# Starts of weight and moving tiles in SBUF: one residue of 256 bytes against all of them for weights

## The chip, the cores and the metric

The kernel runs on one core of a Trainium2 chip. The metric is the device time of one execution in microseconds (us). PE is TensorE, DVE is VectorE, ACT is ScalarE, POOL is GpSimd; SP issues DMAs. PEld is the weight load that precedes each matmul; on its row of the profile it lies beside the matmuls.

## The reference

Three stages in float32, each on the output of the one before:

```python
# q, k, v: 4 batches x 12 heads x 448 x 64
scores = scale * np.matmul(q, k.transpose(0, 1, 3, 2)) - np.log(S)
attn = 1.0 / (1.0 + np.exp(-scores))
x = np.matmul(attn, v)                     # then laid out as 1792 x 768
h = np.maximum(np.maximum(x @ w1, x @ w2), x @ w3)     # 768 x 768 each
y = h @ moe_w_out                                      # 768 x 768
z = y @ w_in                                           # 768 x 2048
g = np.maximum(z, 0.0) + alpha * np.minimum(z, 0.0)
out = g @ moe2_w_out                                   # 2048 x 768
```

## The kernel before

Everything is held transposed: a tile has 128 features on the partitions and 448 tokens along them. Attention (L563 and L584) runs first, as 64x64 tiles of float32. All that follows, 3,528 matmuls at L694, is one form: a weight block of 128x128 and a moving block of 128x448.

Two things make these blocks. First, each product of block matrices is done in Strassen's manner (the Winograd form): sums and differences of weight quarters and of token quarters are formed on VectorE, and seven products k = 0 to 6 take the place of eight. Second, each operand is cut into a high part (a rounded copy, name ending in h) and a low part (the rest, in l), both float32r, and a product is three matmuls: low weights by high moving, high by low, high by high. `split_ops` (L296) makes the pair, `product` (L855) and `e_group` (L1255) issue the matmuls. Weight parts are `f` (made from `weights`, 128x384 for three blocks), `cf` (stored in attention's time and loaded back, for `moe_w_out`) and, in the last stage, `lf`. Moving parts are `x`, `h`, `y` and, in the last stage, `rf`. The matmuls up to about 641 us on the profile's clock are the middle stages (names `u_`), the rest the last one (`eX`, `eV`, `eW`).

Vector and scalar work is not issued where it is written but by a list of operations: `advance` is called after each group of matmuls and issues what is ready and has credit. Its rules are numbers of columns, not addresses.

Where the tiles lie is what the change is about. Pools are stacks in SBUF, from the left (constants, `wpool`, then `slots_a`, in whose place `slots_l` comes for the last stage) and from the right (`edge`, then attention's `apool`, in whose place `slots_c` and then `slots_e` come). Tiles of 448 float32 are 1,792 bytes (7 x 256), tiles of 384 are 1,536 bytes (6 x 256), and a block of 128 inside one is 512 bytes further on. So with the pads of `pad` (L97: 48 words ahead of the first slot of `slots_a`, 16 words behind the slots on the right, 48 words ahead of the moving tiles of `slots_l`) every weight block of L694 starts at byte 0 and every moving block at byte 192, counted modulo 256. Attention's operands all start at byte 0.

`wslot` (L111) gives the 21 buffers of tag `ws` in turn: words as loaded, sums, and `f` and `cf` parts. `tile_l` (L1064) gives the tiles of the last stage, the sixteen of tag `lf` among them; the last stage's even-numbered weight parts come from `wslot`, its odd ones from tag `lf`. A pool that takes the place of another (`reuse_waits="tile"`) makes an instruction wait for the last use of the tiles that its own tile lies over.

Of the kernel before, what the change touches and what calls it, by code (L numbers as in the profile page):

```python
# [16 lines left out]
P = 128  # L17
# [45 lines left out]
def kernel(  # L63
# [19 lines left out]
    HF = HK * P  # L83
# [6 lines left out]
    wpool = ctx.enter_context(tc.tile_pool(name="wpool", bufs=1))  # L90
    dpool = ctx.enter_context(tc.tile_pool(name="store", bufs=1, space=bass.MemoryType.DRAM))
    pools = {}
# [4 lines left out]
    def pad(pool, w):  # L97

        if pool not in padded:
            padded.add(pool)  # L100
            pools[pool].tile([P, w], F32, tag="pad", name=f"pad_{pool}")

    def slot(nm, pool="a", w=TW, dt=F32):
        if pool == "a":
            pad(pool, 48)
        t = pools[pool].tile([P, w], dt, tag="s" + pool, name=nm, bufs=room[pool])
        if pool != "a":
            pad(pool, 16)
        return t

    def wslot(nm, dt=F32, pool="w"):  # L111

        if pool != "w":
            return slot(nm, pool, HF, dt)
        return wpool.tile([P, HF], dt, tag="ws", name=nm, bufs=21)

# [134 lines left out]
    def word_ops(z, gate=None, early=False):  # L253
# [4 lines left out]
        def first():  # L258
            st["r"] = wraw.pop(z)
            st["T"] = wslot(f"wt{z}", U32)  # L260
            if not early:
                nc.scalar.activation(  # L262
                    st["T"].bitcast(F32), st["r"][:, :, 1].bitcast(F32), AF.Abs, scale=2.0**-112
                )
            nc.scalar.activation(st["r"][:, :, 0], st["r"][:, :, 0], AF.Copy, scale=2.0**-29)  # L265
# [53 lines left out]
    def words_via(z):  # L319


        d = dpool.tile([P, HF], F32, tag=f"wv{z}", name=f"wv{z}")

        stored = store_word(z, lambda: d)

        def back(gate):
            def load():
                word[z] = wslot(f"wb{z}")
                nc.sync.dma_start(out=word[z], in_=d)

            return op("Q", 0, load, stored, gate=gate, lag=2)

        return back

    def unit_ops(u, z, gates=None, words=word_ops, store=False, engine="A"):
# [10 lines left out]
        def sum1():  # L346
            t["s"] = wslot(f"wu{u}")
            tensor_op(t["s"], word[z + 2], word[z + 3], ALU.add)
# [65 lines left out]
    def forms(q, of, into, homes, soon=False):  # L414
# [10 lines left out]
        def cut(c, x, *deps):  # L425
            def make(y):
                if y == "h":
                    home[c] = homes(c, 2)
                    take(home[c], 2)
                    if into is hf:  # L430
                        hhome[g, c, r] = home[c]
                return slot(f"{q}_{c}{y}", home[c], TW, F32R)

            o = split_ops(
                into[g, c, r], make, lambda: b[x][0], TW, *deps, gate=lambda: homes(c, 2), soon=soon
            )
            if (c, x) not in ((2, "T"), (1, "21")):
                o.after.append(lambda: used(x))
            return o

        def t1():
            p = homes(None, 1)
            take(p)
            b["T"] = slot(f"{q}_t", p), p
            tensor_op(b["T"][0], b["12"][0], b["11"][0], ALU.subtract)
            used("11")
# [610 lines left out]
    def ff3(ps_m, dpool, fd, wd, slopes, seq, turn_left):  # L1057
# [3 lines left out]
        lf, rf = ({(k, kp): {} for k in range(7 * n) for kp in range(KP)} for n in (1, 2))  # L1061
        sums, held, firsts, pair = {}, {}, [], {}

        def tile_l(tag, nm, w, bufs, dt=F32):  # L1064
            return pools["l"].tile([P, w], dt, tag=tag, name=nm, bufs=bufs)

        def load_op(homes, make, src, gate, lag):
# [23 lines left out]
        def load_w(k, kp, n):  # L1091


            nm = f"wl{k}_{kp}_{n}"

            def make(h):
                if h == "wr":
                    if kp % 2 == 0:
                        pair[kp // 2] = wpool.tile([P, HF, 2], F32, tag="wr", name=nm, bufs=4)
                    x = pair[kp // 2].rearrange("p f t -> p (f t)")  # L1100
                    return x[:, kp % 2 * HF : (kp % 2 + 1) * HF]
                if h == "wf":
                    x = wpool.tile([P, HF, 2], F32, tag="wr", name=nm, bufs=4)
                    return x.rearrange("p f t -> p (f t)")[:, :HF]
                return wslot(nm) if h == "ws" else tile_l("wl", nm, HF, 4)

            def gate():
                if k == 0:
                    return kp // 2 in pair if kp % 2 else free["wr"] > 1
                return "l" in pools  # L1110

            return load_op(("wr",) if k == 0 else ("wl", "ws", "wf"), make, lambda: wd[kp, n], gate, 8 if k else 2)

        def load_g(n, kp, what):
            nm = f"gl{n}_{kp}_{what[0]}{what[1]}"
            key = what, n % 2, kp
            return load_op(

                ("rr", "e") if n else ("a",),
                lambda h: tile_l("rr", nm, TW, 14) if h == "rr" else slot(nm, h),  # L1120
                lambda: fd[key], lambda: (not n or "l" in pools) and key in fd,
                8 if n else 1,
            )
# [4 lines left out]
        def left_ops(k, kp):  # L1128

            if k == 2:  # L1130
                (a, o, end_a), (b, p, end_b) = load_w(k, kp, 1), load_w(k, kp, 3)
                c = sums[kp] = {}

                def add():
                    c["x"] = tile_l("wsum", f"ws{kp}", HF, KP)
                    tensor_op(c["x"], a["x"], b["x"], ALU.add)

                o = op("D", HF, add, o, p, lag=2)
                end_a(o), end_b(o)
            elif k == 3:  # L1140
                (a, o, end_a), (c, p, end) = load_w(k, kp, 0), load_w(k, kp, 1)
                s = sums[kp]
                sums[k, kp] = sum_op(s, s, a, ALU.subtract, HF, o, maker[id(lf[2, kp])])
                o = sum_op(c, a, c, ALU.subtract, HF, p, sums[k, kp])
                end_a(o)
            elif k == 4:
                c, o = sums[kp], sums[3, kp]
            else:
                c, o, end = load_w(k, kp, (0, 2, None, None, None, 3, 2)[k])
                if k == 6:  # L1150
                    o = sum_op(c, c, sums[kp], ALU.subtract, HF, o)
# [261 lines left out]
```

## Time and profile before

| | |
|---|---|
| median of 2 runs | 851.16 us (850.94 to 851.38) |
| profiled execution | 851.17 us, span of the trace 849.3 us |
| PE busy | 844.4 us (99%) |
| PEld busy | 732.8 us (86%) |
| DVE, ACT, POOL busy | 655.4, 517.7, 146.9 us (77, 61, 17%) |
| HBM traffic | 200 GB/s over the span |

In the page's second part each digit is the busy tenth of a fortieth of the span: PE stands at 9 throughout but for the last slice, and so does the granted clock. The chain of work that ended last is followed back from the last instruction to what released it. A busy PE is not PE at its peak, because ends of matmuls are modelled; what tells the pace is the distance from one start to the next.

### The profile page before, as it was taken

How to read it: one execution, taken by the hardware profiler on the slowest of the kernel's cores; microseconds unless marked ns; L12 is line 12 of the kernel's file. 1: busy time of each engine (PE TensorE's matmuls, PEld its weight loads, DVE VectorE, ACT ScalarE, POOL GpSimd, SP SyncE). 2: the span in 40 equal slices, each digit the busy share in tenths (PEclk: the TensorE clock that was granted, in tenths of full speed). 3: DMA queues.
4: the chain of work that ended last, by engine and by line, in shares of the span. 5: the costliest groups of instructions: out<-in, count | busy, mean ns of one | idle time of the engine just before them, and what ended most of it. 6: DMA issues, size and time to landing. Idle time of an engine off the chain costs nothing.

```text
span 849.3 us, 14230 instructions
## 1 busy us (share of the span) xinstructions
PE 844.4 (99%) x4878; PEld 732.8 (86%) x4878; DVE 655.4 (77%) x1304; ACT 517.7 (61%) x1006; POOL 146.9 (17%) x272
## 2 busy tenths in 40 slices
PE   9999999999999999999999999999999999999998
PEld 4444678999999999999999999999999999999997
DVE  1889888789979988797488988977768687868631
ACT  6888997644655464656377867776657554453530
POOL 1464000003200312410001322221211010001110
PEclk9999999999999999999999999999999999999999
DMA  7899632445845765987531766534547999437111
GB/s 269 277 371 350 214 110 87 131 135 191 284 155 159 240 207 171 360 314 222 157 95 65 243 196 232 184 131 155 172 162 265 328 351 371 144 118 242 69 44 54
DMA packets 77863, 170.45 MB, mean 201 GB/s; under 512 B 11120, under 2 KB 51856, under 8 KB 77792
## 3 DMA queue, kind: packets, MB, share of 16 engines
q1 hardware_dynamic: 60048, 106.38, 39.7%
q0 software_dynamic: 17456, 62.83, 19.6%
q8 instruction: 38, 0.62, 0.3%
q10 hardware_dynamic: 288, 0.34, 0.1%
q14 instruction: 33, 0.27, 0.1%
HBM read 123.12 MB, written 46.40 MB: 200 GB/s over the span
## 4 chain that ended last, share of the span: by engine, by line
PE 99%; DVE 0%; ACT 0%; issue 0%
PE u_0X L694 17%; PE u_1X L694 17%; PE eW L694 10%; PE eX L694 10%; PE u_1W L694 9%; PE u_0W L694 9%; PE sc L563 8%; PE pav L584 7%; PE u_0V L694 4%; PE u_1V L694 4%; PE eV L694 3%; PE warm L629 0%; DVE o L1232 0%; ACT o L1230 0%; DVE zeros L625 0%
## 5 line engine op out<-in xcount | busy, mean ns | idle before, releaser
L571 ACT ACTIVATE a<-sc,bias_s 128x896 f32<-128x896 f32 x84 | 83.2, 1010 | 12.7 <-PE sc L563 11.6
L563 PE MATMUL sc<-qt,kt 64*64 64x448 f32 x672 | 83.1, 540 | 0.0
L584 PE MATMUL pav<-a,vt 64*64 64x448 f32 x672 | 82.0, 536 | 0.0
L281 DVE CUSTOM_DVE_ANT_0 wt<-wr,wt 128x768 uint16<-128x768 uint16 x112 | 62.6, 559 | 3.9
L273 DVE SCALAR_TENSOR_TENSOR wr<-wr 128x384 uint32<-128x384 uint32 x112 | 62.0, 554 | 0.4
L265 ACT ACTIVATE wr<-wr 128x384 uint32<-128x384 uint32 x112 | 62.1, 554 | 0.0
L563 PEld LDWEIGHTS sc<-qt,kt 64*64 64x64 f32 x672 | 36.3, 134 | 29.3 <-issue 14.8
L584 PEld LDWEIGHTS pav<-a,vt 64*64 64x64 f32 x672 | 35.9, 133 | 28.1 <-issue 19.1
L262 ACT ACTIVATE wt<-wr 128x384 f32<-128x384 f32 x92 | 51.0, 554 | 14.7 <-DMA wr<-in_weights_dram 11.6
L741 DVE SCALAR_TENSOR_TENSOR r<-n,nalpha,r 128x448 f32<-128x448 f32 x64 | 42.8, 682 | 14.5 <-ACT n L738 14.4
L774 POOL DMA_DIRECT2D gd<-r x48 | 25.9, 541 | 159.6 <-DVE r L741 145.2
L245 POOL DMA_DIRECT2D wd<-wt x32 | 17.7, 553 | 174.4 <-DVE wt L281 173.6
L889 ACT COPY u<-u_1X 128x448 f32<-128x448 f32 x40 | 21.3, 533 | 38.5 <-PE u_1X L694 38.4
L272 DVE TENSOR_SCALAR wt<-wt 128x384 uint32<-128x384 uint32 x112 | 39.8, 355 | 5.5 <-ACT wt L262 4.8
L889 ACT COPY u<-u_0X 128x448 f32<-128x448 f32 x40 | 21.3, 533 | 35.6 <-PE u_0X L694 35.5
L874 ACT COPY u_0V<-u_0X 128x448 f32<-128x448 f32 x20 | 10.3, 518 | 48.0 <-PE u_0X L694 48.0
L311 DVE TENSOR_TENSOR u<-u_1W,u 128x448 f32<-128x448 f32 x34 | 21.2, 623 | 23.8 <-ACT u L889 19.5
L311 DVE TENSOR_TENSOR u<-u_0W,u 128x448 f32<-128x448 f32 x34 | 21.2, 623 | 18.3 <-ACT u L889 14.4
L1287 ACT COPY p<-eW 128x448 f32<-128x448 f32 x12 | 6.4, 534 | 34.1 <-PE eW L694 34.1
L599 DVE COPY x<-pav 128x448 f32<-128x448 f32 x12 | 7.5, 624 | 22.3 <-PE pav L584 22.3
L737 ACT ACTIVATE r<-u 128x448 f32<-128x448 f32 x32 | 18.5, 579 | 5.6 <-DVE u L311 5.6
L311 DVE TENSOR_TENSOR p<-eX,p 128x448 f32<-128x448 f32 x12 | 7.5, 623 | 16.4 <-PE eX L694 16.4
(821 smaller groups left out, 2791.7 us busy)
## 6 DMA issues: line engine op xcount, KB each, us to landing
wr<-in_weights_dram SPq DMA_DIRECT2D x100, 384.0 KB, 3.6
gl<-gd SPq DMA_DIRECT2D x79, 224.0 KB, 4.4
wl<-wd SPq DMA_DIRECT2D x64, 192.0 KB, 4.5
gd<-r POOLq DMA_DIRECT2D x48, 224.0 KB, 2.7
gl_T<-gdT SPq DMA_DIRECT2D x32, 224.0 KB, 5.1
hr<-hd POOLq DMA_DIRECT2D x28, 224.0 KB, 5.9
wd<-wt POOLq DMA_DIRECT2D x32, 192.0 KB, 3.8
kt<-in_k_dram SPq DMA_DIRECT2D x23, 224.0 KB, 5.3
```

The lines of the kernel that those rows point to most:

```text
L262: nc.scalar.activation(st["T"].bitcast(F32), st["r"][:, :, 1].bitcast(F32), AF.Abs, scale=2.0**-112)
L265: nc.scalar.activation(st["r"][:, :, 0], st["r"][:, :, 0], AF.Copy, scale=2.0**-29)
L272: nc.vector.tensor_scalar(st["T"], st["T"], 3, None, ALU.logical_shift_left)
L273: nc.vector.scalar_tensor_tensor(out=st["r"][:, :, 0], in0=st["r"][:, :, 1], scalar=0x80000000, in1=st["r"][:, :, 0], op0=ALU.bitwise_and, ...
L281: nc.vector.tensor_tensor(out=st["T"], in0=st["r"][:, :, 0], in1=st["T"], op=ALU.add)
L311: nc.vector.tensor_tensor(out=out, in0=a, in1=b, op=op)
L563: nc.tensor.matmul(sc[g * KH : (g + 1) * KH, j, :S], keys[u, z][r, m * KH : (m + 1) * KH], queries[u, z][r], start=True, stop=True,)
L571: nc.scalar.activation(a, sc[:, :, :S], AF.Sigmoid, bias=bias_s, scale=scale)
L584: nc.tensor.matmul(pv[key][j * D : (j + 1) * D, :S], vts[u][r, m, j], a[r, j], start=start, stop=stop,)
L694: nc.tensor.matmul(ps[:, : rh.shape[-1]], lt, rh, start=(start and z == 0), stop=(stop and z == len(mms) - 1), skip_group_check=True,)
L741: nc.vector.scalar_tensor_tensor(out=s["r"], in0=s["n"], scalar=nalpha[:, f : f + 1], in1=s["r"], op0=ALU.mult, op1=ALU.add,)
L889: nc.scalar.copy(side[u, g, k], banks[X][:, :TW])
```

## The change

Tiles of tag `ws` and of tag `lf` become 8 words (32 bytes) longer, and what is used of such a tile begins at word 0, 1, ... 7 in turn, by a counter that all of them share. With the longer tiles the buffers themselves begin at all multiples of 32 bytes modulo 256, so that the 128-column weight blocks of L694 begin at all multiples of 4 bytes, a quarter of them at multiples of 16. The pads are altered: moving blocks begin at byte 64 in the middle stages and at byte 96 in the last. What is computed, by which instructions and in which order, stays. Attention's operands still begin at byte 0.

```diff
--- before.py
+++ after.py
@@ -102,17 +102,25 @@
 
     def slot(nm, pool="a", w=TW, dt=F32):
         if pool == "a":
-            pad(pool, 48)
+            pad(pool, 40)
         t = pools[pool].tile([P, w], dt, tag="s" + pool, name=nm, bufs=room[pool])
         if pool != "a":
-            pad(pool, 16)
+            pad(pool, 48 if pool == "c" else 40)
         return t
+
+    turn = [0]
+
+    def shifted(pool, tag, w, dt, nm, bufs):
+
+        c = turn[0] % 8
+        turn[0] += 1
+        return pool.tile([P, w + 8], dt, tag=tag, name=nm, bufs=bufs)[:, c : c + w]
 
     def wslot(nm, dt=F32, pool="w"):
 
         if pool != "w":
             return slot(nm, pool, HF, dt)
-        return wpool.tile([P, HF], dt, tag="ws", name=nm, bufs=21)
+        return shifted(wpool, "ws", HF, dt, nm, 21)
 
 
 
@@ -1062,6 +1070,8 @@
         sums, held, firsts, pair = {}, {}, [], {}
 
         def tile_l(tag, nm, w, bufs, dt=F32):
+            if tag == "lf":
+                return shifted(pools["l"], tag, w, dt, nm, bufs)
             return pools["l"].tile([P, w], dt, tag=tag, name=nm, bufs=bufs)
 
         def load_op(homes, make, src, gate, lag):
```

No row changes its place on any engine. What differs are some waits, because tiles of the last stage lie over other tiles of the middle stages than before. The place that tells most is SP's queue where the last stage's pool is taken into use (`gl` are stored activations, `wl` weight words, both loaded back for the last stage; in square brackets the semaphores, PE_49 being PE's). Before:

```order
L1084 DMA gl1_0_00_7529<-gd00_1_0_5370 128x448 [waits DMAHW1_49,PE_49]
L1084 DMA gl1_1_00_7534<-gd00_1_1_5696 128x448 [waits DMAHW2_49]
L1084 DMA gl1_2_00_7539<-gd00_1_2_5989 128x448 [waits DMASW4_49,DMAHW3_49,DMASW2_49,DVE_49]
L1084 DMA gl1_3_00_7544<-gd00_1_3_6292 128x448 [waits DMAHW4_49]
L1084 DMA gl1_4_00_7549<-gd00_1_4_6573 128x448 [waits DMAHW5_49,DMASW0_49]
L1084 DMA gl1_5_00_7554<-gd00_1_5_6850 128x448 [waits DMAHW6_49,DMASW2_49]
L1084 DMA gl1_6_00_7559<-gd00_1_6_7119 128x448 [waits DMAHW0_49,DMAHW7_49,DMASW4_49,DVE_49]
L1084 DMA gl1_7_00_7564<-gd00_1_7_7347 128x448 [waits DMASW4_49]
...
L1084 DMA wl1_6_2_7622<-wd62_5654 128x384 [waits DMAHW7_49]
L1084 DMA wl1_7_2_7631<-wd72_6118 128x384 [waits DMAHW0_49]
L1084 DMA wl2_2_1_7812<-wd21_2474 128x384 [waits DMAHW5_49]
```

After the change:

```order
L1094 DMA gl1_0_00_7529<-gd00_1_0_5370 128x448 [waits DMAHW1_49,PE_49]
L1094 DMA gl1_1_00_7534<-gd00_1_1_5696 128x448 [waits DMAHW2_49,DMAHW5_49,DVE_49,PE_49]
L1094 DMA gl1_2_00_7539<-gd00_1_2_5989 128x448 [waits DMAHW3_49]
L1094 DMA gl1_3_00_7544<-gd00_1_3_6292 128x448 [waits DMAHW4_49,DMASW4_49,DMASW2_49]
L1094 DMA gl1_4_00_7549<-gd00_1_4_6573 128x448 [waits DMASW0_49]
L1094 DMA gl1_5_00_7554<-gd00_1_5_6850 128x448 [waits DMAHW6_49,DMASW2_49]
L1094 DMA gl1_6_00_7559<-gd00_1_6_7119 128x448 [waits DMAHW7_49,DMASW4_49,PE_49]
L1094 DMA gl1_7_00_7564<-gd00_1_7_7347 128x448 [waits DMAHW0_49,DMASW4_49]
...
L1094 DMA wl1_6_2_7622<-wd62_5654 128x384 [waits DMAHW7_49,PE_49]
L1094 DMA wl1_7_2_7631<-wd72_6118 128x384 [waits DMAHW0_49,PE_49]
L1094 DMA wl2_2_1_7812<-wd21_2474 128x384 [waits DMAHW5_49,PE_49]
```

Before, the one wait for PE is that of gl1_0, and it is for the last matmul of u16_0W. With the change, the program's counts say, gl1_0 waits for a matmul of u16_0V, 18 counts earlier, five more loads wait for PE, each for a later count than the one before it, and the last, wl2_2, for the same count as gl1_0 before.

## Rows read from the trace of the kernel before

**Rows 1.** The page: busy us and share by engine; the chain that ended last.
```profile
PE 844.4 (99%) x4878; PEld 732.8 (86%) x4878; DVE 655.4 (77%) x1304; ACT 517.7 (61%) x1006; POOL 146.9 (17%) x272
...
PE 99%; DVE 0%; ACT 0%; issue 0%
```

**Rows 2.** Waits of PE: who for whom, us in total, times, longest.
```profile
PE warm L629 <- DVE zeros L625: 1.2, 1, 1.2
```

**Rows 3.** Timeline of the end, all engines: start, length, instruction.
```profile
845.26 0.37 PE L694 MATMUL eW<-rf_7h,lf_7h 128*128 128x448 f32 x1
845.66 0.35 ACT L1230 COPY o<-eW 128x224 f32<-128x224 f32 x1 [26.92 <-PE eW L694]
...
846.04 0.39 DVE L1232 COPY o<-eW 128x224 f32<-128x224 f32 x1 [4.61 <-ACT o L1230]
846.46 0.34 SPq L1225 DMA_DIRECT2D out_dram<-o  x1
```

**Rows 4.** The chain in order of time: start, length, line, instructions.
```profile
1.22 2.74 PE warm L629 x6
...
127.47 0.75 PE sc L563 x8
128.22 0.75 PE pav L584 x8
...
467.06 3.64 PE u_1W L694 x18
...
641.78 29.12 PE eX L694 x144
...
758.26 58.24 PE eX L694 x288
```

**Rows 5.** The page, costliest groups: attention matmuls, count, busy us, mean ns.
```profile
L563 PE MATMUL sc<-qt,kt 64*64 64x448 f32 x672 | 83.1, 540 | 0.0
L584 PE MATMUL pav<-a,vt 64*64 64x448 f32 x672 | 82.0, 536 | 0.0
```

**Rows 6.** Stretches: us; busy us of PE, PEld, DVE, ACT, POOL; clock, DMA share, GB/s.
```profile
75.00:230.00 155.00, 155.00 (x1093) 127.41 (x1086) 133.49 (x277) 109.28 (x197) 19.13 (x35) 1.00 0.54 174
230.00:480.00 250.00, 250.00 (x1238) 231.73 (x1237) 202.87 (x399) 144.88 (x306) 38.65 (x71) 1.00 0.61 197
580.00:750.00 170.00, 170.00 (x842) 157.61 (x841) 129.46 (x244) 100.08 (x210) 19.49 (x36) 1.00 0.69 237
```

**Rows 7.** Timeline of PE where attention ends.
```profile
131.91 0.47 PE L694 MATMUL u_0X<-x_0h,f_0l 128*128 128x448 f32 x1
132.23 0.36 PE L694 MATMUL u_0X<-x_0l,f_0h 128*128 128x448 f32 x1
132.43 0.36 PE L694 MATMUL u_0X<-x_0h,f_0l 128*128 128x448 f32 x1
132.63 0.37 PE L694 MATMUL u_0X<-x_0l,f_0h 128*128 128x448 f32 x1
132.83 0.56 PE L694 MATMUL u_0X<-x_0h,f_0h 128*128 128x448 f32 x2
```

**Rows 8.** Timeline of the weight loads at the same place.
```profile
132.23 0.19 PEld L694 LDWEIGHTS u_0X<-x_0h,f_0l 128*128 128x128 f32 x1
132.43 0.19 PEld L694 LDWEIGHTS u_0X<-x_0l,f_0h 128*128 128x128 f32 x1
132.63 0.39 PEld L694 LDWEIGHTS u_0X<-x_0h,f_0h 128*128 128x128 f32 x2
```

**Rows 9.** Last stage, tile eX: count, ns min/median/max, first and last start.
```profile
L694 PE MATMUL eX<-rf_0h,lf_0l x18: 367/368/368, 641.6 to 811.5; 128*128 128x448 f32 x18
L694 PEld LDWEIGHTS eX<-rf_0l,lf_0h x18: 187/188/188, 641.6 to 811.5; 128*128 128x128 f32 x18
L694 PE MATMUL eX<-rf_0l,lf_0h x18: 361/361/361, 641.8 to 811.7; 128*128 128x448 f32 x18
...
L694 PE MATMUL eX<-rf_0h,lf_0h x18: 363/363/363, 642.0 to 811.9; 128*128 128x448 f32 x18
```

**Rows 10.** The page, DMA issues: count, KB each, median us to landing.
```profile
wl<-wd SPq DMA_DIRECT2D x64, 192.0 KB, 4.5
...
wd<-wt POOLq DMA_DIRECT2D x32, 192.0 KB, 3.8
```

**Rows 11.** Waits on SP's DMA queue: us in total, times, longest.
```profile
SPq L1084 <- PE u_0W L694: 21.0, 1, 21.0
```

## The prediction

> **What bounds the kernel now.** I read the share of busy time first: PE is busy for 844.4 of 849.3 us [rows 1]. A busy share can hide waits, so the list of waits came next: the only thing that PE ever waited for is the zeroing of its warm-up block, 1.2 us at the start [rows 2]. The chain of work that ended last then says the same of the end: PE holds 99% of it [rows 1], and behind the last matmul, which starts at 845.26 us, only two copies of 0.35 and 0.39 us and the output's last transfers remain [rows 3]. So the time is a sum of matmul spacings, and an edit counts only if it alters the spacing, or if it makes PE wait where it does not now.
>
> Which spacings? In attention the chain shows eight matmuls in 0.75 us, again and again [rows 4]. From 131.91 us on [rows 7] all 3,528 matmuls (the 4,878 of rows 1 less twice 672 of attention [rows 5] and 6 of the warm-up [rows 4]) are of one form, 128x128 weights against 448 columns. The chain gives 18 in 3.64 us in the middle, 144 in 29.12 and 288 in 58.24 us in the last stage [rows 4]: 202.2 ns each, the same everywhere, whatever VectorE, ScalarE and the DMAs do meanwhile. 3,528 x 202.2 = 713.4 us, and 131.9 + 713.4 = 845.3 us, where the last one begins. The sum closes; there is no other term.
>
> The granted clock is 1.00 in these stretches [rows 6], that is the 2.4 GHz level. 448 columns at 2.4 GHz are 186.7 ns, so 15.5 ns of each spacing (54.7 us in all) are not columns. Two views say what they might be. A weight load begins with each matmul and runs under it: the loads stand at the same hundredths of a us as the matmuls before theirs, 132.23, 132.43, 132.63 [rows 7, 8]. And the recorded matmul durations come in a beat of three, 368, 361 and 363 ns for the three products of a triple, hardly a ns of spread in 18 of each [rows 9]. Durations here are spacing plus a constant, so their distances from their mean, 364, put the spacings at an estimated 206.2, 199.2 and 201.2 ns. Nothing outside PE has such a beat. I read it as the stream of moving columns and the stream of weights getting in each other's way, at phases that repeat because every weight row begins at byte 0 and every moving row at byte 192, counted modulo 256.
>
> **The change part by part.** Order and number of instructions stay. (1) Attention's tiles keep their addresses (they are laid from the other end of the memory), so its 131.9 us stay: 0. (2) Moving rows still begin at one residue each, 64, in the last stage 96. (3) Weight rows begin at any word. Parts 2 and 3 act on one number, the mean spacing, 3.53 us of the total for each ns. The kernel before has one pair of residues only, so no row shows another, and the price has to be bounded. From below: 186.7 ns, no excess left, -54.7 us, 796.5 us; a floor, since every last stall would have to come from these addresses. From above: the heaviest step of the beat every time, 206.2 ns, 4.0 x 3.528 = +14.1 us, 865 us; no row excludes more, since no word-shifted row is in the trace. Between these ends the nearest rows are the first spacings of the stage, before the beat has settled: the starts 132.23, 132.43, 132.63 and 132.83 [rows 7] are three spacings in 0.60 us, 200 ns with an error of some 3 ns from the hundredths. A phase off the beat thus costs about what the beat costs, and I take 202.2 ns: 0 us.
>
> The Trainium skill speaks against part 3: SBUF — State Buffer, Specifications, gives cachelines of 16 bytes and a penalty for each cross to a new line. Three quarters of the word starts are off a 16-byte line, and a 512-byte weight row from there touches 33 lines and not 32; as an estimate from that page, a 32nd of the 15.5 ns in three quarters of the loads is 0.36 ns, or +1.3 us. No row of the kernel before has such a load.
>
> (4) Other engines and DMAs read and write the shifted tiles. What hides a loss there is that PE waits for none of them. In the densest stretch, 75 to 230 us, VectorE is busy 133.5 of 155 us [rows 6]; its work would have to grow by 16% before it binds by busy time. DMAs of weights land in some 4 to 5 us [rows 10]; if their cover went, the loss would be such a landing at the head of a stage, a few us. I put 0. (5) The new addresses move some waits, since a tile of the last stage now lies over other tiles of the stage before. On SP's queue gl1_0 waits 21.0 us for a matmul on u_0W [rows 11], with all further loads queued behind it. In the change's program the wait of gl1_0 is for an earlier matmul; gl1_1, gl1_6, wl1_6 and wl1_7 wait for later ones in turn, and the old one stands 36 rows further on, at wl2_2. So SP's loads go out no later than now, and nobody on the path waited for them: 0.
>
> Sum: 849.3 us of span + 0, and 851.17 - 849.3 = 1.9 us around it: 851 us. The profiled execution (851.17) is as good as the median of the two shown (851.16).
>
> **The rivals.** Faster, the beat breaks to the good. For it: the heavy step returns every third time because nothing varies; with varied starts the dear phase might be left. If only the other two steps remained, the mean were 200.2 ns, -7.1 us, 844 us; if half of the 15.5 ns went, -27 us, 824 us. Against it: the unsettled spacings are no cheaper than the rest by more than their error [rows 7]. It decides below 197.4 ns, where 17 us (2%) are gained.
>
> Slower, shifted weight loads stall the stream more. For it: a fixed pattern can be one that has settled into few collisions, and shifted rows never let it settle. The heavy step every time gives 865 us; 868 us need 207.0 ns, 4.8 over now, a third more stall than today. Against it: the mean would have to pass the worst step on record.
>
> Nothing happens: the address does not matter, and the 15.5 ns are the load's own pace; 851 us with the same beat of 368, 361, 363 ns. For it: loads of 187 to 188 ns [rows 9] that start with the matmul before end close to the next one's start, and the beat is the same for all tiles, wherever in memory they lie. Against it: a plain hand-over between load and matmul has no reason to repeat only after three. The Trainium skill has this as a rule (SBUF — State Buffer, Who interferes with whom): PE reads the moving operand and the weights over two independent ports and never waits on anyone. By it the change does nothing; the trace, 202.2 against 186.7 ns, agrees only if the excess is no conflict.
>
> **How the numbers follow.** Mean spacing as now within about 1.5 ns, in another beat: 0.44 (846 to 856 us). No effect whatever: 0.10. Faster by more than that: 0.27, of which 0.17 beyond 2%. Slower by more: 0.19, of which 0.12 beyond 2% (shifted DMAs that at last make PE wait are in it with 0.03). Two per cent are about what a measurement of this kernel can tell from no change. So faster 0.17, same 0.44 + 0.10 + 0.10 + 0.07 = 0.71, slower 0.12. For the range I cut 0.10 on either side: 828 us (195.6 ns) to 870 us (207.5 ns).
>
> **What would show it.** In the chain's rows after: eight attention matmuls still in 0.75 us; 144 matmuls of the last stage in 29.1 us if I am right, in 28.4 or less for the faster rival at 2%, in 29.8 or more for the slower. The three durations should no longer be 368, 361 and 363 with hardly a spread: if they are, the third rival holds. Moving rows at 64 and at 96 should differ little, middle and last stage keeping one mean. PE's list of waits should still hold the 1.2 us of the warm-up alone; a DMA or VectorE there would make steps 4 or 5 wrong. A mean more than 5 ns off 202 would make the step from three unsettled spacings to "a phase off the beat costs the same" the wrong one.

## The result: 0.6% slower, and every added microsecond is matmul spacing

| | before | after |
|---|---|---|
| median | 851.16 us | 856.61 us |
| ratio to before | | 1.0063, 95% interval 1.0043 to 1.0083 |
| span of the profiled execution | 849.3 us | 854.7 us |

Forecast were 851 us and no change. By the medians the kernel became 5.45 us slower. That is only 0.6%, but the interval lies wholly above 1. The prediction took two per cent for about what a measurement of this kernel can tell from no change; this one tells 0.2% to either side.

The page after the change, part 1, and its chain by engine (they answer to [rows 1]):

```profile
PE 849.7 (99%) x4878; PEld 731.8 (86%) x4878; DVE 655.7 (77%) x1304; ACT 518.9 (61%) x1006; POOL 147.1 (17%) x272
...
PE 99%; DVE 0%; ACT 0%; issue 0%
```

PE's waits in the same trace (they answer to [rows 2]):

```profile
PE warm L637 <- DVE zeros L633: 1.2, 1, 1.2
```

So PE still waits for nothing after its warm-up. VectorE's busy time went from 655.4 to 655.7 us; reading and writing tiles that start at odd words cost it nothing that shows.

The chain in order of time, of attention's end and of the last stage (start, length, line, number of matmuls; it answers to [rows 4]):

```profile
128.97 0.75 PE sc L571 x8
...
645.51 29.26 PE eX L702 x144
674.77 29.28 PE eV L702 x144
704.05 58.67 PE eW L702 x288
762.72 58.99 PE eX L702 x288
821.71 29.25 PE eW L702 x144
```

Attention keeps its 0.75 us for eight, and the first matmul of the long part starts at 131.90 us, a hundredth before where it did (timeline; it answers to [rows 7]):

```profile
131.90 0.47 PE L702 MATMUL u_0X<-x_0h,f_0l 128*128 128x448 f32 x1
```

The last stage shows what changed: 144 matmuls in 29.26 us (203.2 ns each), 288 in 58.67 (203.7) and in 58.99 (204.8), where 29.12 and 58.24 stood everywhere [rows 4]. The one number 202.2 has become several.

The last instructions (timeline; they answer to [rows 3]):

```profile
850.58 0.36 PE L702 MATMUL eW<-rf_7h,lf_7h 128*128 128x448 f32 x1
850.98 0.35 ACT L1240 COPY o<-eW 128x224 f32<-128x224 f32 x1 [27.03 <-PE eW L702]
...
851.36 0.39 DVE L1242 COPY o<-eW 128x224 f32<-128x224 f32 x1 [4.62 <-ACT o L1240]
```

From the first of the long part's matmuls to the last it was 845.26 - 131.91 = 713.35 us [rows 3, 7]; now it is 850.58 - 131.90 = 718.68 us. 5.33 us over 3,527 spacings are 1.51 ns for each; the mean went from 202.25 to 203.77 ns (202.22 and 203.74 without the first spacing, which is 313 and 307 ns; all means below leave it out). The span grew by 5.4 us. Nothing is left for a wait, a load or another engine.

Durations of the same matmuls of tile eX (count, ns min/median/max; they answer to [rows 9]):

```profile
L702 PE MATMUL eX<-rf_0h,lf_0l x18: 362/367/371, 645.3 to 816.6; 128*128 128x448 f32 x18
...
L702 PE MATMUL eX<-rf_0l,lf_0h x18: 362/363/365, 645.5 to 816.8; 128*128 128x448 f32 x18
...
L702 PE MATMUL eX<-rf_0h,lf_0h x18: 362/367/372, 645.7 to 817.0; 128*128 128x448 f32 x18
```

The beat of 368, 361, 363 ns without a spread is gone: each product now varies by 3 to 10 ns. The addresses do reach the pace of PE, which settles that rival at once. What remained to be found was why the mix is dearer than the one fixed pair.

### The profile page after: what moved, and what is told of

Its sections match the earlier page's. It is cut to its first block, busy times and chain, and to the rows that moved or that the text cites. A ratio compares the mean times of both kernels' runs of the same rounds, so it can differ in the third digit from the quotient of the medians.

```text
span 854.7 us, 14234 instructions
## 1 busy us (share of the span) xinstructions
PE 849.7 (99%) x4878; PEld 731.8 (86%) x4878; DVE 655.7 (77%) x1304; ACT 518.9 (61%) x1006; POOL 147.1 (17%) x272
## 4 chain that ended last, share of the span: by engine, by line
PE 99%; DVE 0%; ACT 0%; issue 0%
PE u_0X L702 17%; PE u_1X L702 17%; PE eX L702 10%; PE eW L702 10%; PE u_1W L702 9%; PE u_0W L702 9%; PE sc L571 8%; PE pav L592 7%; PE u_1V L702 4%; PE u_0V L702 4%; PE eV L702 3%; PE warm L637 0%; DVE o L1242 0%; ACT o L1240 0%; DVE zeros L633 0%
## 5 line engine op out<-in xcount | busy, mean ns | idle before, releaser
L571 PE MATMUL sc<-qt,kt 64*64 64x448 f32 x672 | 95.2, 541 | 0.0
L592 PE MATMUL pav<-a,vt 64*64 64x448 f32 x672 | 94.2, 537 | 0.0
L571 PEld LDWEIGHTS sc<-qt,kt 64*64 64x64 f32 x672 | 39.2, 134 | 31.5 <-issue 21.4
L592 PEld LDWEIGHTS pav<-a,vt 64*64 64x64 f32 x672 | 39.5, 133 | 28.0 <-issue 21.6
```

The lines of the kernel that those rows point to most:

```text
L571: nc.tensor.matmul(sc[g * KH : (g + 1) * KH, j, :S], keys[u, z][r, m * KH : (m + 1) * KH], queries[u, z][r], start=True, stop=True,)
L592: nc.tensor.matmul(pv[key][j * D : (j + 1) * D, :S], vts[u][r, m, j], a[r, j], start=start, stop=stop,)
```

## Experiments, first part: which of the two moves costs

Three theories. **Settling:** with fixed starts the two streams fall into a short repeating beat that is cheaper than what a changing start gets. **Alignment:** a weight row that starts off a multiple of 16 bytes costs more. **Moving row:** 64 and 96 are worse places than 192.

Only the moving blocks moved:

```diff
-            pad(pool, 48)
+            pad(pool, 16)
...
-            pad(pool, 16)
+            pad(pool, 48 if pool == "c" else 40)
...
-                        pad("l", 48)
+                        pad("l", 24)
```

> Only the moving blocks are moved (64, in the last stage 96); every weight block stays at byte 0. Settling theory (fixed residues let the two streams fall into a short repeating beat that is cheaper than a generic phase): a beat of three or so again, mean spacing 202.2 ns within 0.5, 850 to 853 us. Alignment theory (a weight row off a multiple of 16 bytes costs more): no such row, 851 us. Moving-row theory (64 and 96 are worse places than 192): 203.8 ns, 856 to 857 us.

Measured: 848.77 us, ratio 0.9973 (0.9963 to 0.9982). Faster, where no theory had it: the middle and the last stage went opposite ways. Chain, a piece of the middle (blocks at 64) and two of the last stage (at 96):

```profile
463.42 3.60 PE u_1W L694 x18
636.22 29.56 PE eX L694 x144
...
754.48 59.14 PE eX L694 x288
```

3.60 us for 18 are 200.0 ns, 29.56 for 144 are 205.3 ns. Both are settled: in the middle stages the single spacings repeat 201, 201, 198 (or 197, 202, 201) to the end, in the last stage a beat of five between 202 and 209 ns. So a fixed pair does settle, but not always cheaply: 64 is better than 192, 96 is worse.

Only the weights spread, moving blocks back at 192:

```diff
-            pad(pool, 40)
+            pad(pool, 8)
...
-            pad(pool, 48 if pool == "c" else 40)
+            pad(pool, 16)
...
-                        pad("l", 48)
+                        pad("l", 8)
```

> Weight blocks at all multiples of 4 as in the change, moving blocks back at 192. Settling theory: 203.8 ns, 856 to 857 us. Alignment theory: 203.8 ns, 856 to 857 us. Moving-row theory: 202.2 ns, 851 us.

Measured: 858.23 us, 1.0084 (1.0069 to 1.0099), mean spacing 204.2 ns from start to start. The spread weights make the loss by themselves; the moving row theory falls.

The shift by words left out, first wholly, then made the same single word for every tile:

```diff
-        c = turn[0] % 8
+        c = 0
```

> As the change, but without the shift by words: weight blocks begin at all multiples of 32 bytes, none off a multiple of 16. Settling theory: the phase still changes from load to load, 203.8 ns, 856 to 857 us. Alignment theory: 202.2 ns, 851 us. Moving-row theory: 203.8 ns, 856 to 857 us.

```diff
-        c = turn[0] % 8
+        c = 1
```

> As the run with multiples of 32, but every weight block one word further on (4, 36, 68, ...): the same steps from load to load, and all loads off a multiple of 16 where the change has three quarters of them. Settling theory: as the run before it, 203.8 ns, 856 to 857 us. Alignment theory: 202.2 + 1.5/0.75 = 204.3 ns, 858 to 859 us, 7 us over the run before it. Moving-row theory: 856 to 857 us.

Measured: 854.76 us, 1.0045 (1.0030 to 1.0060), for multiples of 32; 857.86 us, 1.0083 (1.0068 to 1.0098), with the word. The matmuls of a stretch of the middle stages, first with multiples of 32, then with one word more (us; busy us of PE with the count, of PEld; clock, DMA share, GB/s):

```profile
133.00:633.00 500.00, 500.00 (x2462) 461.85 (x2461) 1.00 0.58 186
```

```profile
133.00:633.00 500.00, 500.00 (x2451) 460.17 (x2450) 1.00 0.58 186
```

500 us by 2,462 are 203.1 ns, by 2,451 204.0 ns. Such a quotient is some 0.15 ns low, because the count takes in the one or two matmuls still running at 133 us; from start to start the middle stages have 203.25 and 204.15 ns. Means over all spacings are 203.18 and 204.18 ns. So multiples of 32 without any misaligned row already lose 1.0 ns against 202.2, which alignment does not explain, and the word adds 1.0 ns, which settling does not explain.

## Experiments, second part: the distance of the two starts

In the trace with multiples of 32, I sorted the spacings by the distance from the start of the weight block that is loading to the start of the moving block that is streaming, modulo 256 (starts in time from the trace, addresses from the program). The middle stages (moving at 64) and the last (at 96) then agreed within 1.1 ns, though the same distance there means another weight address: 201.6 and 201.3 ns at distance 64, 205.3 and 205.0 at 96, all others between 202.0 and 203.8. These are means; within each distance the single spacings scatter by some 3 ns. With the run that moved only the moving blocks, in which 64 gave 200.0 and 96 gave 205.3 ns, this is a fourth theory, to be tried with fixed distances. **Distance:** each distance has its own price.

Moving blocks at 64 everywhere, weights at 0:

```diff
-            pad(pool, 48)
+            pad(pool, 16)
...
-            pad(pool, 16)
+            pad(pool, 48 if pool == "c" else 48)
...
-                        pad("l", 48)
+                        pad("l", 16)
```

> Weight blocks at byte 0 as before, moving blocks at 64 in all stages. The trace with multiples of 32 and the one with only the moving blocks moved agree in one thing: the spacing goes with the distance from a weight block's start to the moving block's, modulo 256; 64 is the cheapest (200.0 ns when it never changes), 96 the dearest (205.3 ns). Distance theory: 200.0 ns in all stages, 7.8 us off, 843 to 844 us. Rival, it was the stage and not the place (the last stage has three matmuls in turn per weight pair and other tiles): the last stage stays near 205 ns, 849 us.

Measured: 844.53 us, 0.9916 (0.9902 to 0.9929), the fastest of all, 6.6 us below the kernel before in the same sessions. The last stage in its chain:

```profile
637.52 28.80 PE eX L694 x144
...
752.72 57.60 PE eX L694 x288
```

28.80 us for 144 are 200.0 ns, as in the middle. It was the place and not the stage. The time is half a microsecond over what was expected. In the profiled execution that lies in attention, which ended later and waited once for a DMA (PE's waits beyond the warm-up, and the first matmul of the long part):

```profile
PE sc L563 <- DMA qt<-in_q_dram: 0.5, 1, 0.5
```

```profile
133.23 0.48 PE L694 MATMUL u_0X<-x_0h,f_0l 128*128 128x448 f32 x1
```

So of the 7.8 us that the spacings save, 133.23 - 131.91 = 1.3 us are lost again before the long part begins.

Weights at 32, moving blocks at 96 in the middle and at 224 in the last stage, so that the distances are 64 and 192:

```diff
-    bias_s = const.tile([P, 32], F32, name="bias_s")[:, :1]
+    bias_s = const.tile([P, 40], F32, name="bias_s")[:, :1]
...
-            pad(pool, 48)
+            pad(pool, 16)
...
-            pad(pool, 16)
+            pad(pool, 40 if pool == "c" else 8)
```

> Weight blocks all at byte 32, moving blocks at 96 in the middle stages and at 224 in the last: the distances 64 and 192. Distance theory: 200.0 ns in the middle, 202.2 in the last stage, 845 to 846 us. Rival, the moving block's own place counts: 205.3 ns in the middle, about 859 us.

Measured: 846.55 us, 0.9943 (0.9930 to 0.9957). Its chain:

```profile
463.90 3.60 PE u_1W L694 x18
636.70 29.12 PE eX L694 x144
```

Moving blocks at 96 cost 205.3 ns with weights at 0 and 200.0 ns with weights at 32; the last stage has the 29.12 us of [rows 4] again, from two other addresses. At these two distances it is the distance that decides, not either start.

The other distances that are multiples of 32, by moving blocks alone, first 128 in the middle with 0 and 160 in the last stage, then 224 with 32 and 64:

```diff
-            pad(pool, 48)
+            pad(pool, 32)
...
-            pad(pool, 16)
+            pad(pool, 32 if pool == "c" else 64)
...
-                        pad("l", 48)
+                        pad("l", 40)
```

> Weight blocks at 0; moving blocks at 128 in the middle stages, in the last stage at 0 (first and second half of the tokens apart: 0 and 160). From the trace with multiples of 32, where distances follow each other at random, distance theory: about 203.4 ns at 128, 202.5 at 0, 203.1 at 160, 854 to 856 us. Settling theory alone (any fixed pair settles into a cheap beat): 200 to 202.2 ns for all three, 844 to 851 us.

```diff
-            pad(pool, 48)
+            pad(pool, 56)
...
-            pad(pool, 16)
+            pad(pool, 8 if pool == "c" else 56)
...
-                        pad("l", 48)
+                        pad("l", 16)
```

> Weight blocks at 0; moving blocks at 224 in the middle stages, in the last at 32 and 64 for the two halves of the tokens. Distance theory: 203.6 ns at 224, 203.5 at 32, 200.0 at 64, about 854 us. Settling theory alone: 200 to 202.2 ns for all, 844 to 851 us.

Measured: 854.73 us, 1.0042 (1.0027 to 1.0057), and 857.17 us, 1.0070 (1.0052 to 1.0089), the second some 3 us over what was expected, because 32 cost 206.5 ns and not 203.5. Windows of the middle stages and pieces of the chain in the last stage, first of the run with 128, 0 and 160:

```profile
133.00:633.00 500.00, 500.00 (x2452) 460.36 (x2451) 1.00 0.58 186
646.83 14.39 PE eX L694 x71
661.42 14.43 PE eX L694 x72
```

then of the run with 224, 32 and 64:

```profile
133.00:633.00 500.00, 500.00 (x2453) 459.58 (x2452) 1.00 0.58 186
646.69 14.87 PE eX L694 x72
661.36 14.40 PE eX L694 x72
```

All eight distances, each held fixed, from these rows and the ones above (length by count; 128 and 224 as the middle stages' means from start to start, because of the windows' counts):

| distance | 0 | 32 | 64 | 96 | 128 | 160 | 192 | 224 |
|---|---|---|---|---|---|---|---|---|
| ns per matmul | 202.7 | 206.5 | 200.0 | 205.3 | 204.0 | 200.4 | 202.2 | 204.0 |

Their mean is 203.1 ns. The spread over multiples of 32 measured 203.18. **So settling is not what the spread lost:** fixed pairs are on average as dear as changing ones. It lost because 192, where the kernel before stood, is one of the cheaper of the list, and the mean over all is 0.9 ns above it. The agreement is one of means: a single distance can cost some 3 ns more or less when it is held than in the spread (32: 206.5 against 203.1 to 203.8 ns; 160: 200.4 against 202.9 and 203.3).

## Experiments, third part: starts between the multiples of 32

```diff
-        c = turn[0] % 8
+        c = 4
```

> As the run with multiples of 32, every weight block 16 bytes further on (16, 48, 80, ...). Alignment to 16 is what the word shift breaks: 203.2 ns as with multiples of 32, 854 to 855 us. Rival, the distance must be a multiple of 32 to be cheap, or the eight distances in between have a dearer list of their own: about 204.2 ns as with one word, 858 us.

```diff
-        c = turn[0] % 8
+        c = 2
```

> As the run with multiples of 32, every weight block 8 bytes further on. If any start off a multiple of 16 costs one more piece of memory per load, this costs as much as one word did: 204.2 ns, 858 us. Rival, one word is dear by its own list of distances: between 203.2 and 203.8 ns, which is what the loads at 8 modulo 16 show in the changed kernel's trace, 855 to 857 us.

Measured: 855.77 us, 1.0048 (1.0033 to 1.0063), mean spacing 203.49 ns, for 16 bytes; 856.81 us, 1.0057 (1.0040 to 1.0074), 203.62 ns, for 8. With 203.18 for none and 204.18 for one word that is no step at 16 bytes: in these traces a shift that keeps every row on a multiple of 16 costs 0.3 ns, one that breaks it by 8 bytes 0.4, by 4 bytes 1.0. The times resolve only the last of these: the intervals for none, 16 and 8 bytes overlap, and that for one word (1.0068 to 1.0098) lies above the first two. The changed kernel's own trace, sorted by the start of the loading weight block modulo 16, has means of 203.25 ns at 0, 204.23 at 4, 203.76 at 8 and 203.75 at 12. Whether these are surcharges or again a list was to be told by holding such distances fixed. The last stage's odd products have room for it: weights at byte 4, 16 and 8 for products 1, 3 and 5, moving blocks at 64 and 160 in one run, at 224 and 32 in the other, the middle stages at distance 64. Only the lines that place the weight parts are shown; the pads that place the moving blocks change besides.

```diff
...
-                return tile_l("lf", nm, HF, 2 * KP, F32R) if k % 2 else wslot(nm, F32R)
+                s = {1: 1, 3: 4, 5: 2}.get(k)
+                return tile_l("lf", nm, HF + 64, 2 * KP, F32R)[:, s : s + HF] if k % 2 else wslot(nm, F32R)
...
```

> Moving blocks at 64, in the last stage at 64 and 160 for the two halves of the tokens (200.0 and 200.1 ns where weights stand at 0). In the last stage the weight parts of the odd products begin all at byte 4 (product 1), at 16 (product 3) and at 8 (product 5): settled distances 60 and 156, 48 and 144, 56 and 152. Alignment theory: 16 costs nothing more (200 to 200.2 ns), 4 and 8 cost about 1 ns more each (201 ns). List theory (each distance has its own price, and a start off 16 bytes is nothing by itself): the six lie anywhere between 200 and 207 ns, the two at 16 bytes as far off 200 as the others. 843 to 846 us in either case.

> As the run before, with moving blocks of the last stage at 224 and 32 (204.0 and 206.6 ns where weights stand at 0): settled distances 220 and 28 (weights at 4), 208 and 16 (at 16), 216 and 24 (at 8). Alignment theory: 204.0 and 206.6 at 16 bytes, 205.0 and 207.6 at 4 and 8. List theory: any of them may be cheaper than at 0; in the traces of spread weights 208, 16 and 24 came out at 202 to 203 ns. 845 to 848 us in either case.

Measured: 846.01 us, 0.9930 (0.9906 to 0.9955), and 848.15 us, 0.9963 (0.9947 to 0.9979). Chain pieces of the first run, in order distance 60 (one word), 48 (16 bytes) and, with one matmul of the row before it, 56 (8 bytes):

```profile
665.80 14.88 PE eV L694 x72
724.15 14.72 PE eW L694 x72
782.63 14.62 PE eX L694 x73
```

and of the second run, distances 208 and 16, both of them 16 bytes off:

```profile
725.18 14.56 PE eW L694 x72
739.75 14.20 PE eW L694 x71
```

206.7, 204.4 and 200.3 ns; 202.2 and 200.0 ns. The others, from the single starts, are 203.5 (156), 204.3 (220) and 201.7 (28) with one word, 204.0 (144) with 16 bytes, 203.2 (152), 202.8 (216) and 202.2 (24) with 8. A row that starts 8 bytes off can be as cheap as 200.3 ns, and one on a multiple of 16 as dear as 204.4, where the alignment theory had 201 and 200: the distances between have a list of their own, and a flat surcharge alone does not make it. That there is no surcharge beside the list is not shown. In every run the moving blocks begin at multiples of 32, so a weight start off a multiple of 16 and a distance off a multiple of 16 always come together; no run moves both blocks off by the same word. By class the four fixed distances mean 204.0 (4 bytes), 202.1 (8) and 202.7 ns (16). That one word is dearest agrees with the spread runs; for 8 and 16 bytes four distances of eight are too few to say more.

One thing in these traces limits the list. Distance 160, in the first of these two runs, from three places in it:

```profile
650.92 14.67 PE eX L694 x71
709.73 14.22 PE eW L694 x71
```

```profile
767.96 14.46 PE eX L694 x70
```

206.6, 200.3 and again 206.6 ns, each held for 70 matmuls or more in a row; a fourth visit, from 826 us, took 206.6 too. The run with 128, 0 and 160 had 200.1 to 200.4 in all its visits. The four visits here all follow blocks at distance 64, so neither the distance nor the one before it tells which of the two beats is entered. Distance 224 has two as well, and in the middle stages of its run the spacing goes from the one to the other at about 350 us and stays there:

```profile
158.11 3.66 PE u_1X L694 x18
...
370.49 3.68 PE u_0X L694 x18
```

3.66 us for 18 are 203.3 ns, 3.68 us 204.4; the 204.0 of the table is a mixture. Each distance off a multiple of 32 was visited once, so a second beat there would not have been seen. With 206.6 in place of 200.4 for 160 the mean of the list were 203.9 ns, so it still would not lie below the spread's.

## Why the prediction was wrong

**What bounds the kernel: right.** The time is the sum of matmul spacings, all of the span's 5.4 us lies in them, and PE's waits stayed at 1.2 us.

**Steps 1, 4 and 5: right at 0.** Attention kept its spacing. VectorE and the DMAs did not reach the path. Of the moved waits the first shows on SP's queue (it answers to [rows 11]):

```profile
SPq L1094 <- PE u_0V L702: 17.5, 1, 17.5
```

17.5 us on u_0V where 21.0 us on u_0W stood, and nobody on PE noticed.

**The step that failed: "a phase off the beat thus costs about what the beat costs", from the three spacings before the beat settles.** Those three spacings lie at other phases in time, but at the same distance of starts, 192. They were no sample of what the change varies. They would have been one if the beat had been a matter of phase alone; the runs show that the pace goes with the distance, in beats from 200.0 to 206.7 ns, and that the kernel before stood at a cheaper one than the mean. The term put at 0 was +1.5 ns, of which 0.96 are the mean over multiples of 32 (203.18 - 202.22) and 0.56 the finer starts (203.74 - 203.18), 3.4 and 2.0 us. Each of these is read from one trace, and the intervals of the two runs overlap (1.0030 to 1.0060 and 1.0043 to 1.0083), so the division is rough; what of the finer part is distance and what a surcharge is open. That the forecast came within 1% of the time is luck as far as this step goes: the mean of the beats happens to lie some 1.5 ns from the one the kernel stood at. The step's own sign of being wrong, a mean more than 5 ns off 202, could not have shown it, since no distance tried lies that far off. The sign that moving rows at 64 and 96 differ little came true (203.71 ns in the middle, 203.81 in the last stage) only because the weights were spread; with weights at 0 the two are 200.0 and 205.3 ns.

**The bounds held.** 203.8 ns lies between 186.7 and 206.2 ns, but the upper one, taken from the heaviest step of one beat, is no bound: distances 32 and 60 hold a mean of 206.5 and 206.7 ns.

**The rivals.** The slower one named the right side and half of the mechanism: "a fixed pattern can be one that has settled into few collisions". The fixed pattern at 192 was cheap, but fixed patterns as such are not. By its time, 856.6 us, the result lies just past the 846 to 856 us that got the most weight, in what this rival was given. The faster one was wrong in sign for this change, and yet had a point: another fixed distance, 64, gives 200.0 ns, near the 200.2 that it took for the beat without its heavy step. The third, that addresses do not matter, falls: 200.0 to 206.7 ns from nothing but starts. The rule of the Trainium skill (SBUF — State Buffer, Who interferes with whom) that PE's two reads are independent and that PE never waits on anyone gave no reason to expect this: the measured spacings depend on how the two starts lie to each other, and the measurement decides. The penalty that the Trainium skill has for crossing 16-byte lines (SBUF — State Buffer, Specifications), from which +1.3 us were estimated, is not told apart from the distances here: the finer starts cost 2.0 us together, and the 200.3 ns at distance 56 show only that a row 8 bytes off need not be dear.

**What stays open.** That the two streams collide in memory is an inference; the runs show the dependence, not the collision. Why 64 is cheap and 32 dear, why distances 160 and 224 have two beats and what chooses between them, whether a start off 16 bytes costs something by itself, and why spread weights cost 204.2 ns with moving blocks at 192 but 203.7 with 64 and 96 is not settled.

## To carry to other kernels

Where PE never waits and its spacing lies above the columns' own time, look at the starts of the weight and the moving blocks: here their distance modulo 256 alone moved each matmul by up to 3%. Hold it fixed, try the eight multiples of 32 with pads, and read the price from several stretches of a hundred matmuls, since a distance can have two. Spreading the starts does not help here: a spread pays about the mean of the list. And a sample that keeps the changed quantity constant, as the unsettled spacings did, says nothing of the change.

## What was not expected of the hardware

At a fixed distance a short beat (three matmuls at 32, 64 and 192, five at 96 and 128) repeats within a nanosecond for hundreds of microseconds, whatever VectorE, ScalarE and the DMAs do. The best pair found, distance 64, makes this kernel 0.84% faster (844.53 us) by three pads; no distance tried held a mean nearer to the columns' own 186.7 ns than 200.0 ns.
